# Interim weight bits held in PSUM, layer-2 groups of 6, 5 and 5 blocks, single-step activations and a wider reciprocal spread in a fused attention and two-layer FFN kernel

## The chip, the cores and the metric

The kernel runs on one core of one Trainium2 chip. The metric is the device time of one execution in microseconds, as the median of several executions. The engines are TensorE (PE in the profile; its weight loads are PEld), VectorE (DVE), ScalarE (ACT), GpSimd (POOL) and SyncE (SP), which issues all the transfers of this kernel. [...]

## What is computed

Attention with a learned relative-position bias, then two feed-forward layers with different activations. Cut to what matters:

```python
scores = scale * q @ k.T + bias          # bias: small MLP of log1p|i-j| / log1p(i)
attn   = softmax(scores)                 # row sums, + 1e-9, then divide
x = (attn @ v)                           # 1152 tokens x 512
h = x @ w_in;  g = h * clip(h + 3, 0, 6) / 6;  x = g @ w_out         # layer 1, d_ff 2048
h = x @ w_in2
P = a0 + a1 h + a2 h^2 + a3 h^3;  Q = 1 + |b0||h| + |b1| h^2
out = (P / (Q + 1e-6)) @ w_out2                                       # layer 2, d_ff 2048
```

The inputs are float64. The kernel gets them as pairs of 32-bit words, so each weight block (128 x 512 numbers) arrives as 128 x 1024 words and has to be turned into float32 by integer operations on its bits.

## The kernel before, in words

**Attention.** Eight heads and two batches in five chunks of queries. TensorE computes bias sums (L418), scores (L450, L465), transposes of the exponentials (L655), the product with v (L485), and two small things per chunk: a transpose of the reciprocals of the row sums (L704) and their spread over 128 partitions (L728, `spread_rc`): per batch eight matmuls of 128 columns against a constant 0/1 matrix `sel`. `x_scaled` (L735) multiplies the attention output by that spread. ScalarE and VectorE share the bias units (table `U_ENG`), the copies out of PSUM (`EV_ENG`, `OUT_ENG`) and one VectorE operation adds bias to the scores (L473).

**Feed-forward layers.** Every float32 operand is split in two parts, high and low, and each product is three matmuls (high*high, high*low, low*high). The 16 blocks of d_ff are handled in groups (`FGROUPS`): layer 1 in groups of 3, 5, 4, 4 blocks, layer 2 in groups of 5, 5, 6. Within a group the three token chunks of 384 tokens follow each other; a step is one block and one chunk, so each layer has 48 steps, numbered 0 to 47 and 48 to 95. A step is: twelve matmuls into a PSUM bank `h` (L317, pool of four banks), the activation, the split of its result (ACT L883, then DVE or POOL L891), and the back product into banks `y` (L962; layer 1 uses four banks of 384 columns, layer 2 three of 512). After a group's last step for a chunk, `y_out` (L988, L990, L992) adds the `y` banks to the sums in SBUF, and at the end of layer 2 sends them out (L994).

**Layer 2's activation**, per step: ACT `abs` L899, `q` L906, `u` L912; POOL `qq` L918; DVE `step_uu` L924 and L925 back to back; ACT logarithm L931 and exponential L936; DVE `step_div` L942, L943, L944 back to back; then ACT L883 and POOL L891. The `h` bank is free again after L944.

**Weights.** An item is one weight block, 64 in all; the fourth block's number of an item is its side (in or out). `w_load` (L794) brings the words into a buffer of the tag `big` (11 of them). `w_bits` makes float32 in three VectorE operations on one tile `wk` in SBUF: L267 reads the high words and writes `wk`; L269 reads the high words and `wk` and writes `wk`; L271 reads the low words and `wk` and writes `wk`. Then ACT L813 makes the high part and POOL L822 the low part, in a home that `w_home` picks: the first four items of a group in one of two `huge` buffers, seven items of the even groups in `wp`, the rest in `big`.

**Order.** The tile framework runs with a manual schedule: a list of small pieces of work (`plan`), each issuing a few instructions, is run through in the order of the table `ORDER`. Every engine works through its own instructions strictly in that order. Buffers and banks are taken from a pool where the piece that needs one is run, and wait for the reader that last held them.

Of the kernel before, what the change touches and what calls it, by code (L numbers as in the profile page):

```python
# [33 lines left out]
FGROUPS = (((0, 3), (3, 8), (8, 12), (12, 16)), ((0, 5), (5, 10), (10, 16)))  # L34
NWP = 7
NPAIR = NH // 2
U_ENG = (0, 0, 1, 0, 0, 0, 1, 0, 1, 0, 0, 0, 1, 0, 0, 0, 0, 0, 1, 0, 0, 0, 0, 0, 0, 0, 0, 0, 1, 0, 0, 0, 0, 0, 1, 0, 0,
# [7 lines left out]
OUT_ENG = (0, 0, 0, 0, 0, 0, 0, 0, 0, 0, 0, 0, 0, 0, 1, 1, 0, 1, 1, 1)  # L45
X_DVE = (0, 0, 0, 0, 1, 0, 0, 0, 1)
PTX = (1,) * 20 + (0,) * 20
N_EARLY = 5
# [1032 lines left out]
```

## Time and profile before

| what | us |
|---|---|
| median of 3 runs | 622.6 (620.86 to 623.19) |
| the profiled execution | 622.65 |
| its span in the profile | 620.9 |
| PE busy | 591.9 |
| DVE busy | 491.8 |
| ACT busy | 397.8 |
| POOL busy | 207.8 |

The profile is of the execution with 622.65 us; 1.75 us of it lie outside the span. "Busy" is the time in which an engine had some instruction under way. Matmuls overlap each other, so the duration of one is longer than the distance from one to the next; where the prediction prices matmuls it takes the length of a run of them. The same holds in a small way for VectorE, whose next operation starts before the row of the last one ends.

### The profile page before, as it was taken

The numbers are of one execution on the slowest core, as the hardware profiler recorded it, in microseconds if no ns is written. First come the engines' busy times: TensorE is split into PE (matmuls) and PEld (weight loads), VectorE is DVE, ScalarE is ACT, GpSimd is POOL, SyncE is SP. The second block draws the span as 40 slices with busy tenths as digits, with TensorE's granted clock in tenths as the row PEclk, the third lists the DMA queues.
The fourth block names the chain that finished last, engine by engine and source line by source line (L and its number), as shares of the span: only waits on it lengthen the run. The fifth ranks groups of instructions, "written<-read, shape, count | busy, mean of one in ns | idle before, by whom it ended". The sixth has DMA issues, their size and how long they took to land.

```text
span 620.9 us, 11361 instructions
## 1 busy us (share of the span) xinstructions
PE 591.9 (95%) x4342; PEld 516.9 (83%) x4342; DVE 491.8 (79%) x926; ACT 397.8 (64%) x833; POOL 207.8 (33%) x184
## 2 busy tenths in 40 slices
PE   8989999999999999999999999979979898969996
PEld 5457777777789999999999999968868787958885
DVE  7978787665767774567576679998999899999973
ACT  6968888887784634233333347668867777567981
POOL 1000100100034533022221213555757856567651
PEclk9999999999999999999999999999979999979999
DMA  7993224124344424072221324301012224000102
GB/s 244 250 231 95 64 59 118 52 77 113 106 114 160 135 78 129 2 235 77 94 68 43 94 96 142 102 34 35 34 35 68 69 93 145 1 1 1 52 28 75
DMA packets 31974, 56.63 MB, mean 91 GB/s; under 512 B 2472, under 2 KB 18984, under 8 KB 31920
## 3 DMA queue, kind: packets, MB, share of 16 engines
q1 hardware_dynamic: 31920, 55.91, 30.3%
q8 instruction: 34, 0.56, 0.4%
q14 instruction: 20, 0.16, 0.1%
HBM read 41.75 MB, written 2.36 MB: 71 GB/s over the span
## 4 chain that ended last, share of the span: by engine, by line
PE 62%; DVE 27%; ACT 4%; DMA 4%; issue 1%; SPq 0%; POOL 0%; ACTq 0%; POOLq 0%
PE h L317 20%; PE y L962 19%; PE h L485 6%; PE h L655 6%; PE ps L450 5%; DVE wk L269 4%; DVE wk L271 4%; PE h L418 4%; DVE e L925 3%; DVE e L944 3%; DVE e L942 3%; DVE h L943 3%; DVE e L924 2%; DVE wk L267 2%; DMA huge<-wk 2%; DMA vraw<-in_v_dram 2%
## 5 line engine op out<-in xcount | busy, mean ns | idle before, releaser
L317 PE MATMUL h<-xt,huge 128*128 128x384 f32 x504 | 95.4, 337 | 0.1
L317 PEld LDWEIGHTS h<-xt,huge 128*128 128x128 f32 x504 | 89.0, 189 | 2.3 <-DVE e L944 0.8
L822 POOL TENSOR_TENSOR huge<-wk,huge 128x512 fp32r<-128x512 f32 x28 | 39.3, 1404 | 98.8 <-ACT huge L813 95.8
L891 POOL TENSOR_TENSOR gl<-e,gh 128x384 fp32r<-128x384 f32 x48 | 50.0, 1041 | 57.9 <-ACT gh L883 52.4
L473 DVE CUSTOM_DVE_ANT_0 big<-ps,huge 128x576 f32<-128x576 f32 (+1 forms) x72 | 52.4, 761 | 17.5 <-PE ps L450 16.1
L269 DVE SCALAR_TENSOR_TENSOR wk<-big,wk 128x512 int32<-128x512 int32 x64 | 63.9, 1004 | 0.7
L317 PE MATMUL h<-xt,big 128*128 128x384 f32 x324 | 62.2, 341 | 2.3 <-DVE e L944 2.3
L918 POOL TENSOR_TENSOR e<-e,e 128x384 f32<-128x384 f32 x48 | 54.7, 1143 | 22.4 <-ACT e L906 22.3
L317 PE MATMUL h<-xt,wp 128*128 128x384 f32 x324 | 60.8, 336 | 1.0 <-DVE e L944 1.0
L317 PEld LDWEIGHTS h<-xt,big 128*128 128x128 f32 x324 | 57.9, 192 | 4.3 <-DVE e L944 3.6
L866 ACT ACTIVATE e<-h,cons 128x384 f32<-128x384 f32 x43 | 25.0, 581 | 55.7 <-PE h L317 55.7
L317 PEld LDWEIGHTS h<-xt,wp 128*128 128x128 f32 x324 | 57.0, 188 | 3.0 <-DVE e L944 1.6
L755 POOL TENSOR_TENSOR xt<-oT,xt 128x512 fp32r<-128x512 f32 x7 | 8.9, 1280 | 145.4 <-ACT xt L749 145.4
L637 ACT ACTIVATE big<-big,mx 128x576 f32<-128x576 f32 (+1 forms) x72 | 56.1, 790 | 2.1 <-DVE mx L473 2.1
L271 DVE SCALAR_TENSOR_TENSOR wk<-big,wk 128x512 int32<-128x512 int32 x64 | 56.2, 884 | 0.2
L883 ACT ACTIVATE gh<-h 128x384 fp32r<-128x384 f32 x43 | 21.1, 492 | 47.7 <-PE y L962 45.8
L411 DVE TENSOR_SCALAR big<-psw,thr 128x576 f32<-128x576 f32 x104 | 47.5, 517 | 2.9 <-PE h L418 2.6
L962 PE MATMUL y<-huge,gh 128*128 128x512 f32 x108 | 34.9, 424 | 12.3 <-DVE part L990 8.5
L883 ACT ACTIVATE gh<-e 128x384 fp32r<-128x384 f32 x48 | 25.1, 523 | 29.1 <-DVE e L944 28.6
L655 PEld LDWEIGHTS h<-csm,big 128*128 128x128 f32 x328 | 35.4, 142 | 10.0 <-issue 7.1
L655 PE MATMUL h<-csm,big 128*128 128x128 f32 x328 | 41.2, 277 | 1.6 <-ACT wk L426 1.2
L418 PE MATMUL h<-big,wblk 128*32 128x288 f32 x576 | 40.7, 410 | 1.9 <-ACT wk L426 0.9
(120 smaller groups left out, 1310.6 us busy)
## 6 DMA issues: line engine op xcount, KB each, us to landing
big<-in_moe_w_in_dram SPq DMA_DIRECT2D x32, 512.0 KB, 4.0
big<-in_moe_w_out_dram SPq DMA_DIRECT2D x32, 512.0 KB, 3.5
huge<-wk SPq DMA_DIRECT2D x40, 288.0 KB, 4.0
kraw<-in_k_dram SPq DMA_DIRECT2D x4, 576.0 KB, 9.4
rawq<-in_q_dram SPq DMA_DIRECT2D x4, 512.0 KB, 6.8
vraw<-in_v_dram SPq DMA_DIRECT2D x8, 256.0 KB, 8.2
out_dram<-part SPq DMA_DIRECT2D x5, 256.0 KB, 2.5
out_dram<-psw SPq DMA_DIRECT2D x3, 256.0 KB, 2.5
```

What stands on the lines that cost most here:

```text
L269: nc.vector.scalar_tensor_tensor(wt, high, -0x40000000, wt, op0=ALU.bitwise_and, op1=ALU.bitwise_or)
L271: nc.vector.scalar_tensor_tensor(wt, low, 29, wt, op0=ALU.logical_shift_right, op1=ALU.bitwise_or)
L317: nc.tensor.matmul(ps, wx[:, c, :], xx[:, c, :], start=(i == c == 0), stop=(i == 2 and c == KC - 1))
L411: eng.tensor_scalar(dst, win, thr[:, g:g + 1], 0.0, op0=ALU.add, op1=ALU.max)
L418: nc.tensor.matmul(ps[32 * ct:32 * ct + 32, :HS], wblk.rearrange("p i h -> p (i h)"), units_of[G, ct][:, hf * HS:(hf + 1) * HS], start=Tru ...
L473: nc.vector.tensor_tensor_reduce(ss, ps, biases[qc][:, h * S:h * S + n], op0=ALU.add, op1=ALU.min, scale=-0.125, scalar=3e38, accum_out=mx)
L637: nc.scalar.activation(ss, ss, AF.Exp, bias=mxs[u // 2][:, b, u % 2:u % 2 + 1], scale=-1.0, accum_out=sums[qc][:, b, h:h + 1])
L655: nc.tensor.transpose(ps[:, c - c0], pes[u][:, c * P:(c + 1) * P], ident)
L883: nc.scalar.activation(gs[j][0], hs[j] if L == 0 and j >= N_EARLY else act[j], AF.Copy)
L891: eng.tensor_tensor(gl, src, gh.bitcast(F32), op=ALU.subtract)
L918: nc.gpsimd.tensor_tensor(vq, vq, ab, op=ALU.mult)
L962: nc.tensor.matmul(ys[c][d][:, :TC if L == 0 else DM], lhs, rhs, start=(first and i == 0), stop=(last and i == 2))
```

## The change

**Interim bits in PSUM.** The first two operations of `w_bits` write a tile `mid`, and only the third writes `wk`. For the six items of the first group `mid` is that same `wk`, as before. For all other items it is a bank of PSUM: one of the four `h` banks up to the fourth item of group 5 (layer 2's second group), from there on one of the four `y` banks, of which layer 2 uses three at a time.

**Groups and homes.** Layer 2's groups are 6, 5, 5. The last two groups keep their last four items in `huge` instead of the first four, and `wp` takes other items.

**Single steps.** `step_uu` is cut into `um` and `uu`, `step_div` into `p`, `r` and `div`; the same five VectorE operations, each with its own place in the order.

**Spread.** `spread_rc` runs per half of the head pairs instead of per batch: four matmuls of 256 columns (both batches) in place of eight of 128. The last chunk has one batch's worth of rows and stays at eight of 128 columns. `x_scaled` follows in halves.

**Order and tables.** `ORDER`, `U_ENG`, `EV_ENG`, `OUT_ENG` and `X_DVE` are new. Of the 144 bias units 33 are on ACT (before 28), of 120 copies of pieces 78 on ACT (before 86). When the first layer-2 step (48) is issued, 40 of the 64 items have their bits made (before 36); the last item's bits come between steps 82 and 83 (before 86 and 87).

```diff
-FGROUPS = (((0, 3), (3, 8), (8, 12), (12, 16)), ((0, 5), (5, 10), (10, 16)))
+FGROUPS = (((0, 3), (3, 8), (8, 12), (12, 16)), ((0, 6), (6, 11), (11, 16)))
-X_DVE = (0, 0, 0, 0, 1, 0, 0, 0, 1)
+X_DVE = (0, 0, 0, 0, 0, 0, 1, 0, 1)
...
-    def to_bits(wt, words, i):
+    def to_bits(wt, mid, words, i):
         low, high = words[:, :, :, 0], words[:, :, :, 1]
         if i == 0:
-            nc.vector.tensor_scalar(wt, high, 3, 0x3FFFFFFF, op0=ALU.logical_shift_left, op1=ALU.bitwise_and)
+            nc.vector.tensor_scalar(mid, high, 3, 0x3FFFFFFF, op0=ALU.logical_shift_left, op1=ALU.bitwise_and)
         elif i == 1:
-            nc.vector.scalar_tensor_tensor(wt, high, -0x40000000, wt, op0=ALU.bitwise_and, op1=ALU.bitwise_or)
+            nc.vector.scalar_tensor_tensor(mid, high, -0x40000000, mid, op0=ALU.bitwise_and, op1=ALU.bitwise_or)
         else:
-            nc.vector.scalar_tensor_tensor(wt, low, 29, wt, op0=ALU.logical_shift_right, op1=ALU.bitwise_or)
+            nc.vector.scalar_tensor_tensor(wt, low, 29, mid, op0=ALU.logical_shift_right, op1=ALU.bitwise_or)
...
+    def in_huge(gi, i):
+        j = i - (0 if gi < 5 else len(items(gi)) - 4)
+        return j if 0 <= j < 4 else None
+
+    def in_wp(gi, i):
+        return (gi == 2 and i >= 4) or (gi == 4 and 4 <= i < 11) or (gi == 6 and 2 <= i < 6)
...
-        def spread_rc(qc, b):
+        def spread_rc(qc, k):
             need(("rcs", qc), "sel")
-            ps = BANK((P, KC, P))
-            for hp in range(NPAIR):
+            n = nb_of(qc)
+            ps = BANK((P, 2, 2, P))[:, :, :n]
+            for e in range(2):
+                hp = 2 * k + e
                 for i in range(2):
-                    nc.tensor.matmul(ps[:, hp], sel[:, hp * P:(hp + 1) * P], rcs[qc][:, i, b], start=(i == 0), stop=(i == 1))
+                    nc.tensor.matmul(ps[:, e], sel[:, hp * P:(hp + 1) * P], rcs[qc][:, i, :n], start=(i == 0), stop=(i == 1))
...
         def w_bits(it, i):
             need(("raw", it), *((("bits", it, i - 1),) if i else ()))
             if i == 0:
-                held["wt", it] = W([P, KC, P], I32)
-            to_bits(held["wt", it], held["raw", it], i)
+                where = "h" if it[0] < 5 or (it[0] == 5 and it[1] < 4) else "y"
+                if where == "y":
+                    need("y")
+                held["mid", it] = W([P, KC, P], I32) if it[0] == 0 else T(pools[where], [P, KC, P], I32, where)
             if i == 2:
-                del held["raw", it]
+                held["wt", it] = held["mid", it] if it[0] == 0 else W([P, KC, P], I32)
+            to_bits(held.get(("wt", it)), held["mid", it], held["raw", it], i)
...
+        def step_um(j):
+            need(("u1", j))
+            nc.vector.tensor_tensor(act[j], act[j], hs[j], op=ALU.mult)
+            done.add(("um", j))
...
+        def step_p(j):
+            need(("exp", j))
+            nc.vector.scalar_tensor_tensor(act[j], act[j], acoef[:, 0:1], hs[j], op0=ALU.add, op1=ALU.mult)
+            done.add(("p", j))
...
-                for i, fn in enumerate((step_abs, step_q, step_u, step_qq, step_uu, step_ln, step_exp, step_div)):
-                    at(t + .1 + .1 * i, fn, j)
+                for i, fn in enumerate((step_abs, step_q, step_u, step_qq, step_um, step_uu, step_ln, step_exp, step_p, step_r, step_div)):
+                    at(t + .1 + .09 * i, fn, j)
```

What this does to VectorE in the middle of layer 2: before, around step 63. `wk` and `big` are in SBUF, `e` is an activation buffer in SBUF, `h` a PSUM bank.

```order
L267 TENSOR_SCALAR wk_5262<-big_5115 128x512
L271 SCALAR_TENSOR_TENSOR wk_5215<-big_5056,wk_5215 128x512
L942 SCALAR_TENSOR_TENSOR e_1013_5191<-e_1013_5191,acoef_59,h_5118 128x384
L943 SCALAR_TENSOR_TENSOR h_5118<-e_1004_5149,h_5118 128x384
L944 SCALAR_TENSOR_TENSOR e_1013_5191<-h_5118,e_1013_5191 128x384
L269 SCALAR_TENSOR_TENSOR wk_5262<-big_5115,wk_5262 128x512
L267 TENSOR_SCALAR wk_5300<-big_5163 128x512
L271 SCALAR_TENSOR_TENSOR wk_5262<-big_5115,wk_5262 128x512
```

The same place after, around step 59. L275, L277, L279 are the three operations on the bits, L947 and L952 the two of `um` and `uu`, L968, L973 and L978 those of `p`, `r` and `div`.

```order
L275 TENSOR_SCALAR y_5062<-big_4876 128x512
L277 SCALAR_TENSOR_TENSOR y_5062<-big_4876,y_5062 128x512
L279 SCALAR_TENSOR_TENSOR wk_5079<-big_4876,y_5062 128x512
L968 SCALAR_TENSOR_TENSOR e_1021_5031<-e_1021_5031,acoef_59,h_4994 128x384
L973 SCALAR_TENSOR_TENSOR h_4994<-e_1023_5035,h_4994 128x384
L947 TENSOR_TENSOR e_1033_5085<-e_1033_5085,h_5038 128x384
L978 SCALAR_TENSOR_TENSOR e_1021_5031<-h_4994,e_1021_5031 128x384
L952 SCALAR_TENSOR_TENSOR e_1033_5085<-e_1033_5085,acoef_59,h_5038 128x384
```

The interim result now lies in a `y` bank, no bit operation has two inputs in SBUF, and the operations of two neighbouring steps alternate.

TensorE at the end of the first chunk of queries, before: the bias sums, the spread, the next scores.

```order
L418 MATMUL h_912<-big_756,wblk_89 32x288 x2
L728 MATMUL h_920<-rcT_863,sel_78 128x128 x8
L728 MATMUL h_934<-rcT_863,sel_78 128x128 x8
L450 MATMUL ps_213_947<-kraw_79,rawq_361 128x288
L450 MATMUL ps_214_948<-kraw_79,rawq_361 128x288
```

And after (L434, L746 and L466 are the same three lines).

```order
L434 MATMUL h_912<-big_751,wblk_89 32x288 x2
L746 MATMUL h_920<-rcT_866,sel_78 128x256 x4
L746 MATMUL h_931<-rcT_866,sel_78 128x256 x4
L466 MATMUL ps_213_939<-kraw_79,rawq_357 128x288
L466 MATMUL ps_214_940<-kraw_79,rawq_357 128x288
```

The spread stands in the same place of the row with half as many matmuls, each twice as wide.

## Rows read from the trace of the kernel before

**Rows 1.** Windows: stretch, its length, busy PE, PEld, DVE, ACT, POOL, PE clock, DMA

```profile
45.00:187.00 142.00, 141.50 (x1721) 107.86 (x1720) 102.13 (x251) 118.33 (x284) 13.03 (x12) 1.00 0.32 90
187.00:385.00 198.00, 198.00 (x1177) 197.61 (x1177) 137.80 (x234) 81.17 (x157) 52.76 (x40) 1.00 0.33 105
385.00:568.00 183.00, 165.52 (x796) 145.66 (x794) 176.38 (x282) 131.45 (x258) 114.53 (x98) 0.96 0.16 52
```

**Rows 2.** Chain of work that ended last: start us, us, what

```profile
190.88 8.55 PE h L317 x48
199.43 2.08 PE y L962 x12
...
385.56 1.39 DVE part L990 x3
...
568.05 2.36 PE h L317 x12
...
593.41 2.10 PE h L317 x12
595.52 2.08 PE y L962 x9
...
614.88 2.05 DVE part L992 x3
```

**Rows 3.** Windows: one of two such of 20 us, columns as in rows 1

```profile
440.00:460.00 20.00, 16.75 (x71) 14.59 (x70) 19.32 (x30) 14.21 (x28) 12.95 (x11) 0.83 0.16 53
```

**Rows 4.** Timeline in layer 2, VectorE and GpSimd: start us, us, what

```profile
560.17 0.60 DVE L942 SCALAR_TENSOR_TENSOR e<-e,acoef,h 128x384 f32<-128x384 f32 x1
...
562.48 1.02 POOL L891 TENSOR_TENSOR gl<-e,gh 128x384 fp32r<-128x384 f32 x1 [1.06 <-ACT gh L883]
562.87 1.18 DVE L269 SCALAR_TENSOR_TENSOR wk<-big,wk 128x512 int32<-128x512 int32 x1
563.45 1.47 POOL L918 TENSOR_TENSOR e<-e,e 128x384 f32<-128x384 f32 x1
563.96 1.24 DVE L267 TENSOR_SCALAR wk<-big 128x512 int32<-128x512 int32 x1
565.12 0.68 DVE L271 SCALAR_TENSOR_TENSOR wk<-big,wk 128x512 int32<-128x512 int32 x1
565.73 0.68 DVE L269 SCALAR_TENSOR_TENSOR wk<-big,wk 128x512 int32<-128x512 int32 x1
...
566.54 1.28 POOL L822 TENSOR_TENSOR wp<-wk,wp 128x512 fp32r<-128x512 f32 x1 [1.63 <-ACT wp L813]
```

**Rows 5.** VectorE's groups between 385 and 568 us: count, busy us, mean ns

```profile
L269 DVE SCALAR_TENSOR_TENSOR wk<-big,wk 128x512 int32<-128x512 int32 x27 | 28.8, 1077 | 0.0
L271 DVE SCALAR_TENSOR_TENSOR wk<-big,wk 128x512 int32<-128x512 int32 x26 | 27.7, 1078 | 0.0
...
L267 DVE TENSOR_SCALAR wk<-big 128x512 int32<-128x512 int32 x27 | 18.0, 680 | 0.0
```

**Rows 6.** Single lines over the whole span: duration ns min/median/max, first and last start

```profile
L267 DVE TENSOR_SCALAR wk<-big x64: 404/418/1509, 164.3 to 564.0; 128x512 int32<-128x512 int32 x64
...
L943 DVE SCALAR_TENSOR_TENSOR h<-e,h x48: 546/553/556, 382.8 to 608.5; 128x384 f32<-128x384 f32 x48
...
L992 DVE SCALAR_TENSOR_TENSOR psw<-y,psw x3: 679/681/684, 575.6 to 579.5; 128x512 f32<-128x512 f32 x3
```

**Rows 7.** The chain of work again, in attention

```profile
67.95 1.93 PE h L728 x16
...
71.05 2.12 PE h L655 x18
```

**Rows 8.** TensorE's waits: whom for, us in total, times, longest

```profile
PE y L962 <- DVE part L990: 8.5, 4, 4.9
PE h L317 <- DVE e L944: 3.3, 4, 1.2
```

**Rows 9.** The page's 40 equal slices of the span: what the transfers moved

```profile
GB/s 244 250 231 95 64 59 118 52 77 113 106 114 160 135 78 129 2 235 77 94 68 43 94 96 142 102 34 35 34 35 68 69 93 145 1 1 1 52 28 75
```

More of the change, by code (lines that the diff above doesn't have):

```diff
@@ L33 @@
 HS = S // 2
-FGROUPS = (((0, 3), (3, 8), (8, 12), (12, 16)), ((0, 5), (5, 10), (10, 16)))
+FGROUPS = (((0, 3), (3, 8), (8, 12), (12, 16)), ((0, 6), (6, 11), (11, 16)))
 NWP = 7
 NPAIR = NH // 2
-U_ENG = (0, 0, 1, 0, 0, 0, 1, 0, 1, 0, 0, 0, 1, 0, 0, 0, 0, 0, 1, 0, 0, 0, 0, 0, 0, 0, 0, 0, 1, 0, 0, 0, 0, 0, 1, 0, 0,
[3 rows of a table removed]
-EV_ENG = (1, 0, 1, 1, 1, 0, 1, 1, 0, 1, 1, 0, 1, 0, 1, 1, 1, 1, 1, 0, 1, 1, 1, 1, 1, 0, 0, 1, 1, 1, 1, 0, 1, 1, 1, 1, 1,
[3 rows of a table removed]
-OUT_ENG = (0, 0, 0, 0, 0, 0, 0, 0, 0, 0, 0, 0, 0, 0, 1, 1, 0, 1, 1, 1)
-X_DVE = (0, 0, 0, 0, 1, 0, 0, 0, 1)
+U_ENG = (0, 0, 1, 1, 0, 0, 0, 0, 1, 1, 0, 0, 0, 0, 0, 0, 1, 1, 0, 0, 0, 0, 0, 0, 0, 0, 1, 0, 0, 0, 0, 0, 0, 0, 1, 0, 0,
[3 rows of a table added]
+EV_ENG = (1, 1, 1, 1, 1, 1, 1, 0, 1, 1, 1, 0, 1, 1, 0, 1, 1, 1, 0, 1, 0, 1, 1, 1, 0, 0, 1, 1, 1, 1, 0, 1, 0, 1, 1, 1, 0,
[3 rows of a table added]
+OUT_ENG = (0, 0, 1, 0, 0, 0, 0, 0, 0, 0, 0, 0, 0, 0, 1, 1, 0, 1, 1, 0)
+X_DVE = (0, 0, 0, 0, 0, 0, 1, 0, 1)
 PTX = (1,) * 20 + (0,) * 20
 N_EARLY = 5
-ORDER = (0, 25, 1, 26, 2, 3, 27, 28, 5, 4, 21, 30, 32, 23, 38, 24, 31, 40, 33, 39, 46, 34, 41, 48, 54, 42, 47, 35, 49,
[115 rows of a table removed]
+ORDER = (0, 25, 1, 23, 24, 26, 2, 3, 27, 28, 4, 5, 21, 30, 32, 38, 31, 33, 39, 40, 46, 34, 48, 41, 47, 318, 49, 35, 54,
[123 rows of a table added]
 NWK = 5
@@ L278, in items @@
         return [(gi, 2 * (f - f0) + s, L * NF + f, bool(s)) for f in range(f0, f1) for s in range(2)]
+    def in_huge(gi, i):
[3 more added lines that the diff above has]
+        return (gi == 2 and i >= 4) or (gi == 4 and 4 <= i < 11) or (gi == 6 and 2 <= i < 6)
     def w_home(gi, i):
-        if i < 4:
-            if i == 0:
+        j = in_huge(gi, i)
+        if j is not None:
+            if j == 0:
                 home[gi] = HUGE([P, 4, 2, KC, P], F32R)
-            return home[gi][:, i]
-        if gi % 2 == 0 and gi > 0 and i < 4 + NWP:
+            return home[gi][:, j]
+        if in_wp(gi, i):
             return T(pools["e"], [P, 2, KC, P], F32R, "wp", bufs=NWP)
@@ L721, in recips_low, with x_scaled @@
             done.add(("rcs", qc))
-        def spread_rc(qc, b):
+        def spread_rc(qc, k):
             need(("rcs", qc), "sel")
-            ps = BANK((P, KC, P))
-            for hp in range(NPAIR):
+            n = nb_of(qc)
+            ps = BANK((P, 2, 2, P))[:, :, :n]
+            for e in range(2):
+                hp = 2 * k + e
                 for i in range(2):
-                    nc.tensor.matmul(ps[:, hp], sel[:, hp * P:(hp + 1) * P], rcs[qc][:, i, b], start=(i == 0), stop=(i == 1))
-            held["bc", qc, b] = ps
-            done.add(("bc", qc, b))
-        def x_scaled(qc, b):
-            need(("bc", qc, b), *(("o", 4 * qc + hp) for hp in range(NPAIR)))
-            o = oT[qc][:, b]
-            nc.vector.tensor_tensor(o, o, held.pop(("bc", qc, b)), op=ALU.mult)
-            done.add(("xs", qc, b))
+                    nc.tensor.matmul(ps[:, e], sel[:, hp * P:(hp + 1) * P], rcs[qc][:, i, :n], start=(i == 0), stop=(i == 1))
+            held["bc", qc, k] = ps
+            done.add(("bc", qc, k))
+        def x_scaled(qc, k):
+            need(("bc", qc, k), *(("o", 4 * qc + hp) for hp in (2 * k, 2 * k + 1)))
+            o = oT[qc][:, :nb_of(qc), 2 * k:2 * k + 2]
+            nc.vector.tensor_tensor(o, o, held.pop(("bc", qc, k)).rearrange("p e b t -> p b e t"), op=ALU.mult)
+            done.add(("xs", qc, k))
         def x_parts(qc, b):
@@ L743, in x_high @@
             c, t = divmod(PLACE[2 * qc + b], 3)
-            need(("xs", qc, b), *((("x room", c),) if t else ()))
+            need(("xs", qc, 0), ("xs", qc, 1), *((("x room", c),) if t else ()))
             if t == 0:
@@ L781, in fused_kernel @@
                 at(t + .16, recips_low, qc)
+                for half in range(2):
+                    at(t + .4 + .03 * half, spread_rc, qc, half)
+                    at(t + .45 + .01 * half, x_scaled, qc, half)
                 for b in range(nb_):
-                    at(t + .4 + .1 * b, spread_rc, qc, b)
-                    at(t + .45 + .1 * b, x_scaled, qc, b)
                     at(t + .5 + .1 * b, x_high, qc, b)
@@ L800, in w_bits @@
             if i == 0:
-                held["wt", it] = W([P, KC, P], I32)
-            to_bits(held["wt", it], held["raw", it], i)
+                where = "h" if it[0] < 5 or (it[0] == 5 and it[1] < 4) else "y"
+                if where == "y":
+                    need("y")
+                held["mid", it] = W([P, KC, P], I32) if it[0] == 0 else T(pools[where], [P, KC, P], I32, where)
             if i == 2:
-                del held["raw", it]
+                held["wt", it] = held["mid", it] if it[0] == 0 else W([P, KC, P], I32)
+            to_bits(held.get(("wt", it)), held["mid", it], held["raw", it], i)
+            if i == 2:
+                del held["raw", it], held["mid", it]
                 done.add(("wt", it))
@@ L809, in w_high @@
             gi, i, n, out_side = it
-            need(("wt", it), *((("home", gi),) if 0 < i < 4 else ()), *(("attention",) if 4 <= i < 4 + NWP and gi % 2 == 0 and gi else ()))
+            need(("wt", it), *((("home", gi),) if in_huge(gi, i) else ()), *(("attention",) if in_wp(gi, i) else ()))
             pair = w_home(gi, i)
@@ L813, in w_high @@
             nc.scalar.activation(pair[:, 0], held["wt", it].bitcast(F32), AF.Copy)
-            if i == 0:
+            if in_huge(gi, i) == 0:
                 done.add(("home", gi))
@@ L919, in step_qq @@
             done.add(("q2", j))
+        def step_um(j):
+            need(("u1", j))
+            nc.vector.tensor_tensor(act[j], act[j], hs[j], op=ALU.mult)
+            done.add(("um", j))
         def step_uu(j):
-            need(("u1", j))
-            u, ps = act[j], hs[j]
-            nc.vector.tensor_tensor(u, u, ps, op=ALU.mult)
-            nc.vector.scalar_tensor_tensor(u, u, acoef[:, 1:2], ps, op0=ALU.add, op1=ALU.mult)
+            need(("um", j))
+            nc.vector.scalar_tensor_tensor(act[j], act[j], acoef[:, 1:2], hs[j], op0=ALU.add, op1=ALU.mult)
             done.add(("u2", j))
@@ L937, in step_exp, with step_r @@
             done.add(("exp", j))
-        def step_div(j):
-            need(("exp", j))
-            u, ps, vq = act[j], hs[j], more[j][1]
-            nc.vector.scalar_tensor_tensor(u, u, acoef[:, 0:1], ps, op0=ALU.add, op1=ALU.mult)
-            nc.vector.scalar_tensor_tensor(ps, vq, 1.0 + 1e-6, ps, op0=ALU.add, op1=ALU.mult)
-            nc.vector.scalar_tensor_tensor(u, ps, -2.0, u, op0=ALU.add, op1=ALU.mult)
+        def step_p(j):
+            need(("exp", j))
+            nc.vector.scalar_tensor_tensor(act[j], act[j], acoef[:, 0:1], hs[j], op0=ALU.add, op1=ALU.mult)
+            done.add(("p", j))
+        def step_r(j):
+            need(("p", j))
+            nc.vector.scalar_tensor_tensor(hs[j], more[j][1], 1.0 + 1e-6, hs[j], op0=ALU.add, op1=ALU.mult)
+            done.add(("r", j))
+        def step_div(j):
+            need(("r", j))
+            nc.vector.scalar_tensor_tensor(act[j], hs[j], -2.0, act[j], op0=ALU.add, op1=ALU.mult)
             done.add(("g", j))
```

250 rows, old and new, of tables (EV_ENG, ORDER, U_ENG) are left out of this document.

## The prediction

> **What bounds the kernel now.** I read the windows first, stage by stage, then the chain of work that ended last, then the timeline where the chain leaves TensorE. In attention and in layer 1 TensorE has no room: it is busy for 141.50 of 142 us and for 198.00 of 198 us [rows 1]. In the next 183 us, up to 568, that turns round: VectorE is busy for 176.38 us and TensorE for 165.52. The chain says the same: TensorE's products back to back from 190.88 on, VectorE from 385.56, TensorE again from 568.05 to the last product at 614.88 [rows 2].
>
> How much TensorE loses there: a step's twelve `h` matmuls and its `y` matmuls take 2.08 us each in layer 1 and 2.10 + 2.08 = 4.19 together in layer 2 (starts of the rows) [rows 2]. From 190.88 there are 47 + 48 such pieces left of layer 1 and 48 pairs of layer 2: 95 x 2.08 + 48 x 4.19 = 398.7 us. They take 614.88 - 190.88 = 424.0. So 25.3 us are lost, and since layer 1 shows no idle time, all of it in layer 2 before 568. [...]
>
> Why VectorE is late: the weight bits. L269 and L271 take 1.08 us on average in that stretch and L267 0.68 [rows 5], but a neighbour of the same shape takes 0.68 where GpSimd is idle [rows 4]. The timeline shows the mechanism: L269 starts at 562.87 beside GpSimd's L891, which ends at 563.50, and ends 0.55 us behind it; L267 starts at 563.96 beside L918, which ends at 564.92, and ends 0.28 us behind it. Each stands until GpSimd's operation is over and then does its work. L943, which has one input in SBUF and one in PSUM, shows nothing of that: 546 to 556 ns over 48 instructions, though GpSimd is busy for 114.53 of the 183 us [rows 1, 6].
>
> **The bits.** The change removes the second SBUF input from L269 and L271 and the SBUF output from L267 and the second operation. What they then cost: the second has L943's operands (SBUF and PSUM in, PSUM out), 552 ns for 384 columns; at 512 columns the like is L992 with PSUM input, 681 ns [rows 6]. Starts of neighbours lie 0.61 us apart for 0.68 us rows [rows 4], so 0.61 each. For the first operation, SBUF in and PSUM out, no row stands: 0.36 from below (404 ns, as it is alone, less the same overlap) and 0.69 from above (L992's whole row); I take 0.60, near the rows with PSUM. An item then costs VectorE 1.82 us. Before it costs, in this stretch, 0.68 + 1.08 + 1.08 less 0.07 overlap each = 2.63 us.
>
> The trace shows no fixed price for PSUM: 681 ns against 680 for two SBUF inputs alone [rows 4, 6]. [...]
>
> **VectorE against TensorE in layer 2.** The five operations of an activation step take 562.87 - 560.17 = 2.70 us from start to start [rows 4]; before and after alike. I count in the order of either kernel what stands between the first layer-2 step on TensorE and the last back product before the bits are all done. Before (up to step 83): 39 steps' worth of activations 105.1, other VectorE work (sums of `y`, second layer's input) 17.7, 28 items x 2.63 = 73.6: 196 us, against 173 us of TensorE (83 pieces of 2.08). The 23 us of surplus answer to the 25.3 lost, so the count can be trusted to some 2 us. After (up to step 80): activations 95, other work 13, 24 items x 1.82 = 43.5: 151.5 us, against 152 us of TensorE (73 pieces). By groups and chunks: 17.9 against 14.6 up to step 47, 21.4 against 25.0 (53), 24.2 against 25.0 (59), 25.2 against 25.0 (65), 20.1 against 20.8 (70), 22.0 against 20.8 (75), 20.7 against 20.8 (80), then VectorE has slack. Only the first piece puts VectorE behind, by 3.3 us, since four items move up to there; the later ones even out. So VectorE stops being the limit, and TensorE is next. I put the loss at 3.3 + 2, about 5 us in place of 25.3: **20.3 us less**. Bounds: 0 us lost (TensorE never waits), 11 if each bit operation costs L992's whole row of 0.69 (24 x 3 x 0.08 = 6 more).
>
> Four of the 28 items go into layer 1: 4 x 1.82 us of VectorE, which is busy there for 137.80 of 198 us [rows 1]; nothing on the path. The bits in layer 1 take one of the four `h` banks for three operations. In layer 2 a step holds its bank over some ten operations of three engines and TensorE still waits for one only 3.3 us in all [rows 8]; in layer 1 a step holds it over four. So a bank is spare there, and the wait costs nothing; without that cover see the last rival. The cut into single steps adds no instruction; it puts other work between operations that depend on each other, a gain or loss of at most the 0.07 us by which rows overlap, taken as nothing.
>
> **The spread.** For the first four chunks of queries it is 16 matmuls of 128 columns, 1.93 us, 121 ns each [rows 7], now 8 of 256. TensorE is full there, so the path feels it. Price of 256 columns: a layer-1 matmul of 384 takes 173 ns [rows 2] and a transpose of 128 takes 118 [rows 7], so 121 from below and 173 from the next wider; 242 if the time grows with the columns. A piece that hardly changes from 118 to 173 between 128 and 384 columns is nearest to 121. 8 x 0.121 = 0.97, a gain of 0.96 x 4 = **3.9 us** (0 to 3.9). The last chunk stays. Other tables (`U_ENG`, `EV_ENG`) trade some operations between ACT (118 of 142 us) and DVE (102 of 142) [rows 1], covered by TensorE.
>
> **The start.** Among SyncE's transfers the last block of k (576 KB) moves behind four more transfers of bias rows, and the 320 KB of the late bias table move ahead of v. The first three slices move 231 to 250 GB/s [rows 9], so the one makes what stands behind it up to 2.4 us earlier and the other 1.3 us later; taken as nothing, 1.5 either way. The new order issues seven `h` pieces ahead of the first back product; TensorE is busy all the same.
>
> **Sum.** 622.65 (the profiled execution, 0.05 above the median) - 20.3 - 3.9 = **598.5 us**.
>
> **The rivals.**
>
> *Banks `y` become the wait.* The interim takes the one `y` bank that layer 2 has spare, and at a change of chunk the next products want it. Before, TensorE waited there for VectorE's sums 8.5 us in four waits, up to 4.9 [rows 8], with the spare bank free. Five changes (59, 65, 70, 75, 80) with 2.1 us each are 10.6: 609 us. For it: VectorE runs at the limit there. Against: the order puts the third bit operation ahead of the new chunk's first product, and VectorE's queue in front of the sums is shorter without the stretched operations. Chance 0.19.
>
> *PSUM costs more.* In layer 2, 48 bit operations now read PSUM, and VectorE is just level with TensorE, so what they cost on top goes into the end. From rows the most is a start distance equal to the whole row, 0.68 - 0.61 = 0.07 each, 3.4 us: 602. Against it: L943 and L992 with PSUM operands are no longer than rows of their width without [rows 4, 6]. Chance 0.04. [...]
>
> *The stretch isn't GpSimd's doing*, but comes from reading every second word of `big`, which stays. Then an item keeps 2.63 us, and 24 x 0.81 = 19.5 us come back: 618. Against: the short rows read `big` in the same way [rows 4]. Chance 0.05.
>
> *Slower: `h` banks in layer 1.* TensorE has no slack there, and 34 items take a bank out of four before step 48. A wait for an `h` bank goes whole into the end. The change's gain of 24.2 us is gone from 24.2 / 34 = 0.71 us of wait per item, little over one bit operation; with two operations, 1.2 us, it is 41 lost: 639. Against: the spare bank above, and VectorE idle for 60 of layer 1's 198 us [rows 1], so that it rarely lets an item wait between its operations. Chance 0.06.
>
> **How the numbers follow.** My forecast has 0.66. Its own range is 593 (no wait at all, and the start's 1.5 not lost) to 606 (12 us lost). The range of 8 in 10 goes to 611, to take in the wait for `y`; it leaves out the last two rivals and some of the edges. Faster by over 0.5%, below 619.5, about the least that a measurement of this kernel can tell from no change: 0.66 + 0.19 + 0.04 and most of the 0.05, 0.92. Within it 0.03, slower 0.05.
>
> **What would show it.** In the new profile: the three bit operations near 0.60 to 0.69 us with little spread, whatever GpSimd does; TensorE's clock full in layer 2 and its lost time between the first `h` and the last `y` at about 5 us; the spread at about 1 us per chunk; attention ending some 4 us earlier, layer 1 as long as before. Wrong would be: bit operations of 1 us and more; waits of `y` products for VectorE of over 8 us; waits of `h` in layer 1.

## The result, and the profile after

The changed kernel takes 599.23 us (median of 4 runs, 598.64 to 599.88), the kernel before 622.19 beside it: a ratio of 0.963, 95% interval 0.961 to 0.966. The forecast was 598.5 us, the range 593 to 611. The total was met; the terms for layer 2 and for the start were not, and it is luck that they cancel. The profiled execution took 599.88 us with a span of 598.1. Lines of code have moved: L269 and L271 are now L277 and L279, L267 is L275, `h` is L333, `y` L996, the spread L746, GpSimd's L891, L918 and L822 are L915, L942 and L846. The experiments have line numbers of their own.

Windows of attention, layer 1 and layer 2 (length, busy PE, PEld, DVE, ACT, POOL, clock, DMA share, GB/s), against [rows 1]:

```profile
45.00:183.00 138.00, 135.31 (x1552) 101.00 (x1552) 98.50 (x243) 110.43 (x261) 9.18 (x9) 0.98 0.33 87
183.00:382.00 199.00, 199.00 (x1290) 196.96 (x1285) 139.12 (x252) 82.68 (x166) 54.89 (x43) 1.00 0.34 109
382.00:560.00 178.00, 178.00 (x911) 163.28 (x910) 163.04 (x306) 149.63 (x293) 114.76 (x108) 1.00 0.18 57
```

Layer 2 is TensorE's now: 178.00 of 178 us at a granted clock of 1.00 (before, 0.83 in the 20 us of [rows 3]), VectorE 163.04. The first row is worse than in [rows 1]: 2.7 us idle and a clock of 0.98.

TensorE's waits over the whole span (line, whom for: us, times, longest), against [rows 8]:

```profile
PE h L434 <- ACT wk L442: 2.7, 5, 0.9
PE h L559 <- POOL ones L383: 2.2, 1, 2.2
PE h L671 <- ACT wk L442: 2.0, 3, 1.1
PE h L501 <- DMA vraw<-in_v_dram: 1.1, 2, 1.0
PE ps L466 <- DMA kraw<-in_k_dram: 1.0, 1, 1.0
PE ps L466 <- DVE mx L489: 0.4, 1, 0.4
```

None of these lines belongs to a layer; all are in the first 50 us. The chain of work says the same (start, us, what), against [rows 2]:

```profile
75.04 1.15 PE h L746 x8
...
197.12 10.82 PE h L333 x60
207.94 6.24 PE y L996 x36
...
581.05 2.10 PE h L333 x12
583.15 8.90 PE y L996 x39
592.05 0.02 issue
592.07 2.05 DVE part L1026 x3
```

From 197.12 TensorE runs unbroken to 592.05: the remaining 46 + 48 pieces of layer 1 and 48 pairs of layer 2 are 94 x 2.08 + 48 x 4.19 = 396.6 us by the prediction's prices, and they take 394.9. Counted to the same mark (the start of the last sum, with 1.4 us of products still to go), the kernel before lost 26.7 us and this one nothing.

The bit operations over the whole span, by the place of their output and of the interim (ns min/median/max, first and last start), against [rows 6]:

```profile
L275 DVE TENSOR_SCALAR h<-big x42: 680/686/689, 206.1 to 457.0; 128x512 int32<-128x512 int32 x42
...
L277 DVE SCALAR_TENSOR_TENSOR h<-big,h x42: 681/689/697, 207.1 to 459.1; 128x512 int32<-128x512 int32 x42
...
L279 DVE SCALAR_TENSOR_TENSOR wk<-big,h x42: 675/682/691, 208.2 to 460.1; 128x512 int32<-128x512 int32 x42
```

And a piece of layer 2's timeline, VectorE and GpSimd, against [rows 4]:

```profile
453.97 0.69 DVE L275 TENSOR_SCALAR h<-big 128x512 int32<-128x512 int32 x1
454.69 0.69 DVE L277 SCALAR_TENSOR_TENSOR h<-big,h 128x512 int32<-128x512 int32 x1
454.93 1.02 POOL L915 TENSOR_TENSOR gl<-e,gh 128x384 fp32r<-128x384 f32 x1 [1.22 <-ACT gh L907]
455.42 0.69 DVE L279 SCALAR_TENSOR_TENSOR wk<-big,h 128x512 int32<-128x512 int32 x1
...
457.01 0.69 DVE L275 TENSOR_SCALAR h<-big 128x512 int32<-128x512 int32 x1
457.36 1.30 POOL L846 TENSOR_TENSOR huge<-wk,huge 128x512 fp32r<-128x512 f32 x1
457.61 0.55 DVE L947 TENSOR_TENSOR e<-e,h 128x384 f32<-128x384 f32 x1
```

L277 ends in the middle of GpSimd's L915; L279 starts in its middle and takes 0.69 us all the same; neither waits for its end. The second L275 starts 0.60 us ahead of its neighbour L947 though L846 begins beside it. Where the three operations of an item follow each other directly, as at the top, their starts are 0.72 and 0.73 us apart and not 0.60; what makes this difference no run shows.

What went the other way is the start. The first spread starts at 75.04 us, before at 67.95 [rows 7]; 7.1 us later. The spreads take 1.15 instead of 1.93 us, so four give back 3.1, and attention ends some 4 us later (counted by the pieces of layer 1 that stand behind it), not 4 us earlier. The place is this (windows, and the chain of work there):

```profile
45.00:50.00 5.00, 2.31 (x16) 1.57 (x15) 1.45 (x4) 2.46 (x7) 0.00 (x0) 0.88 1.04 222
50.00:55.00 5.00, 5.00 (x29) 3.63 (x29) 2.74 (x6) 2.38 (x5) 0.00 (x0) 0.50 0.06 22
```

```profile
39.65 7.79 DMA huge<-wk
...
49.24 2.18 PE h L671 x9
51.42 2.22 PE ps L466 x8
53.64 3.31 PE h L501 x40
56.95 1.13 PE h L671 x9
58.08 1.17 PE ps L466 x8
...
63.30 2.33 PE h L501 x40
```

ScalarE's copy L442 waits until a transfer of bias rows (`huge<-wk`) has given back its buffer `wk`, and TensorE waits for ScalarE. TensorE is busy for 2.31 of 5 us, and then works at a granted clock of 0.50 (50 to 55 us). The same pieces at a clock of 1.00 (56 to 63 us and on) are 1.13, 1.17 and 2.33 us (the last three rows): some 1.0 us each lost, 3.1 together.

### The profile page after: what moved, and what is told of

It is laid out like the page before. It is cut to its first block, busy times and chain, and to the rows that moved or that the text cites. A ratio compares the mean times of both kernels' runs of the same rounds, so it can differ in the third digit from the quotient of the medians.

```text
span 598.1 us, 11410 instructions
## 1 busy us (share of the span) xinstructions
PE 583.8 (98%) x4310; PEld 513.1 (86%) x4310; DVE 460.1 (77%) x930; ACT 397.0 (66%) x830; POOL 195.4 (33%) x184
## 4 chain that ended last, share of the span: by engine, by line
PE 91%; DMA 5%; DVE 3%; ACT 1%; issue 0%; SPq 0%; ACTq 0%; DVEq 0%
PE h L333 34%; PE y L996 33%; PE h L501 7%; PE h L671 6%; PE ps L466 5%; DMA huge<-wk 4%; PE h L434 3%; DVE big L427 2%; PE h L746 1%; PE ps L481 1%; DMA psw<-in_cpsi_dram 1%; PE h L720 0%; DVE part L1026 0%; ACT wk L442 0%; PE ps L474 0%
## 5 line engine op out<-in xcount | busy, mean ns | idle before, releaser
L333 PE MATMUL h<-xt,huge 128*128 128x384 f32 x504 | 94.5, 336 | 0.0
L333 PEld LDWEIGHTS h<-xt,huge 128*128 128x128 f32 x504 | 88.4, 188 | 2.0 <-DVE wk L896 0.3
L333 PE MATMUL h<-xt,big 128*128 128x384 f32 x360 | 67.6, 335 | 0.0
L846 POOL TENSOR_TENSOR huge<-wk,huge 128x512 fp32r<-128x512 f32 x28 | 36.7, 1311 | 88.9 <-DVE h L896 69.6
L942 POOL TENSOR_TENSOR e<-e,e 128x384 f32<-128x384 f32 x48 | 49.1, 1023 | 50.2 <-ACT e L930 49.9
L333 PEld LDWEIGHTS h<-xt,big 128*128 128x128 f32 x360 | 63.1, 188 | 0.8
L915 POOL TENSOR_TENSOR gl<-e,gh 128x384 fp32r<-128x384 f32 x48 | 48.9, 1020 | 23.9 <-ACT gh L907 17.9
L333 PE MATMUL h<-xt,wp 128*128 128x384 f32 x288 | 53.8, 335 | 0.0
L333 PEld LDWEIGHTS h<-xt,wp 128*128 128x128 f32 x288 | 50.7, 188 | 1.1
L896 DVE SCALAR_TENSOR_TENSOR h<-e,h 128x384 f32<-128x384 f32 x43 | 24.0, 559 | 29.5 <-ACT e L890 29.5
L466 PE MATMUL ps<-kraw,rawq 64*128 64x288 f32 x256 | 41.4, 438 | 1.3 <-DMA kraw<-in_k_dram 1.0
L434 PE MATMUL h<-big,wblk 128*32 128x288 f32 x576 | 39.5, 410 | 2.8 <-ACT wk L442 2.7
L968 DVE SCALAR_TENSOR_TENSOR e<-e,acoef,h 128x384 f32<-128x384 f32 x48 | 29.3, 610 | 14.5 <-ACT h L963 14.3
L442 ACT ACTIVATE wk<-h,csm 128x288 f32<-128x288 f32 x72 | 32.1, 493 | 10.5 <-PE h L434 5.0
```

Of the source, the lines that this page charges most:

```text
L333: nc.tensor.matmul(ps, wx[:, c, :], xx[:, c, :], start=(i == c == 0), stop=(i == 2 and c == KC - 1))
L434: nc.tensor.matmul(ps[32 * ct:32 * ct + 32, :HS], wblk.rearrange("p i h -> p (i h)"), units_of[G, ct][:, hf * HS:(hf + 1) * HS], start=Tru ...
L466: nc.tensor.matmul(ps[e][:, 512 - HS * (1 - c):512 + HS * c] if c else ps[e][:, 512 - HS:512], x[r, b, hp, :], kraw[r, hp, S * b + HS * c: ...
L846: nc.gpsimd.tensor_tensor(lo, held.pop(("wt", it)).bitcast(F32), hi.bitcast(F32), op=ALU.subtract)
L915: eng.tensor_tensor(gl, src, gh.bitcast(F32), op=ALU.subtract)
L942: nc.gpsimd.tensor_tensor(vq, vq, ab, op=ALU.mult)
```

## The experiments

All are edits of the changed kernel, but for e2 and e8, which are built on the kernel before. The ratio is to the kernel before in the same comparison, with its 95% interval. The last column is the difference of that ratio and the changed kernel's 0.9632, times 622.2 us; each is uncertain by some 2 us.

| run | median, us | ratio to before | against the changed kernel, us |
|---|---|---|---|
| e1_sbuf | 611.62 | 0.983 (0.980 to 0.986) | +12.3 |
| e2_psum_alone | 636.36 | 1.023 (1.020 to 1.026) | +37.0 |
| e3_start | 591.71 | 0.951 (0.949 to 0.953) | -7.6 |
| e4_narrow | 602.44 | 0.969 (0.966 to 0.971) | +3.4 |
| e5_no_gpsimd | 597.89 | 0.959 (0.957 to 0.962) | -2.4 |
| e6_fused | 603.45 | 0.968 (0.965 to 0.970) | +2.8 |
| e7_psit | 597.33 | 0.958 (0.956 to 0.961) | -3.0 |
| e8_old_layer2 | 622.49 | 1.000 (0.998 to 1.002) | +22.8 |
| e9_engines | 599.51 | 0.962 (0.959 to 0.965) | -0.7 |
| e10_l1_sbuf | 598.74 | 0.961 (0.957 to 0.964) | -1.6 |
| e11_coef | 594.99 | 0.955 (0.952 to 0.958) | -5.1 |
| e12_loads | 592.54 | 0.950 (0.948 to 0.953) | -8.0 |

**e1: the bits back in SBUF.**

```diff
...
-                held["mid", it] = W([P, KC, P], I32) if it[0] == 0 else T(pools[where], [P, KC, P], I32, where)
+                held["mid", it] = W([P, KC, P], I32)
             if i == 2:
-                held["wt", it] = held["mid", it] if it[0] == 0 else W([P, KC, P], I32)
+                held["wt", it] = held["mid", it]
```

> The changed kernel with one edit: the interim bits of every weight go back into an SBUF buffer (wk) instead of a PSUM bank; order, groups, single steps and spread stay. Theory (VectorE's bit operations stretch when GpSimd works beside them and all their operands lie in SBUF): in layer 2 the first and third bit operations take 1.0 to 1.1 us again in the mean instead of 0.68, TensorE loses 15 to 27 us there, and the time is 614 to 626 us. Rival (the new order and the groups of 6, 5, 5 gave the time back, the place of the bits is incidental): the operations may stretch, but the time stays at 598 to 603 us.

Neither: +12.3 us, between the two. VectorE's groups from 382 to 560 us (count, busy us, mean ns):

```profile
L277 DVE SCALAR_TENSOR_TENSOR wk<-big,wk 128x512 int32<-128x512 int32 x24 | 26.2, 1094 | 0.3
L279 DVE SCALAR_TENSOR_TENSOR wk<-big,wk 128x512 int32<-128x512 int32 x24 | 24.5, 1020 | 0.1
...
L275 DVE TENSOR_SCALAR wk<-big 128x512 int32<-128x512 int32 x23 | 17.8, 779 | 0.0
```

The window of the same stretch:

```profile
382.00:560.00 178.00, 168.25 (x840) 150.94 (x839) 171.99 (x286) 136.97 (x271) 120.53 (x100) 0.99 0.17 55
```

The operations stretch as they did before [rows 5], and TensorE is busy for 168.25 of these 178 us instead of 178.00. So the banks do what they were thought to do, but they are worth 12 us in this order, not all of the 26.7.

**e5: the same without GpSimd beside the bits.**

On top of e1's edit:

```diff
...
-            nc.gpsimd.tensor_tensor(lo, held.pop(("wt", it)).bitcast(F32), hi.bitcast(F32), op=ALU.subtract)
+            held.pop(("wt", it))
+            ws[n, out_side] = hi, hi
...
-            nc.gpsimd.tensor_tensor(vq, vq, ab, op=ALU.mult)
```

> The kernel of e1 (interim bits in SBUF, 611.6 us, bit operations of 779, 1112 and 1020 ns in layer 2) with GpSimd's work in the two layers left out: the low halves of all weights and of layer 2's gated values are not subtracted, TensorE reads the high half in their place (same number of matmuls), and the square in layer 2's activation is not taken. VectorE's and ScalarE's instructions are the same. Theory (the operations stretch since GpSimd works beside them on SBUF): the three take 0.40 to 0.45, 0.66 to 0.70 and 0.66 to 0.70 us with hardly any spread, TensorE does not wait in layer 2, and the time is 597 to 600 us. Rival (operands in SBUF are slow for these operations by themselves, as three passes over words of 8 bytes): they stay above 0.9 us, and the time at 607 us or more.

The same groups as in e1:

```profile
L279 DVE SCALAR_TENSOR_TENSOR wk<-big,wk 128x512 int32<-128x512 int32 x24 | 16.4, 684 | 0.1
L277 DVE SCALAR_TENSOR_TENSOR wk<-big,wk 128x512 int32<-128x512 int32 x24 | 16.4, 686 | 0.3
L275 DVE TENSOR_SCALAR wk<-big 128x512 int32<-128x512 int32 x23 | 9.6, 419 | 0.0
```

```profile
382.00:560.00 178.00, 178.00 (x911) 163.28 (x910) 158.20 (x307) 148.00 (x295) 0.00 (x0) 1.00 0.17 55
```

All in SBUF, and no stretch: 0.69 and 0.68 us instead of 1.09 and 1.02, 0.42 instead of 0.78. TensorE is busy for 178.00 of 178 us. The stretch is GpSimd's doing, not the step of 8 bytes in `big`; that rival falls.

**e2 and e8: banks without the new layer 2.** e2 is the kernel before with banks. e8 has the changed kernel's start and layer 1, and the kernel before's layer 2, with banks. What both edit in `w_bits` of the kernel before (which bank `where` names differs: e2 leaves eight items of layer 2's first group in SBUF, e8 gives every item behind the first group a bank):

```diff
-                held["wt", it] = W([P, KC, P], I32)
-            to_bits(held["wt", it], held["raw", it], i)
...
+                held["mid", it] = T(pools[where], [P, KC, P], I32, where) if where and it[0] else W([P, KC, P], I32)
             if i == 2:
-                del held["raw", it]
+                held["wt", it] = W([P, KC, P], I32) if it in banked else held["mid", it]
...
+            to_bits(held.get(("wt", it)), held["mid", it], held["raw", it], i)
```

> The kernel before with one part of the change: the interim bits of 44 of its 58 weight items after the first group go into PSUM banks or stay there where a bank is free (groups 2 to 4 of layer 1 and groups 2 and 3 of layer 2, and the last two out-side items of layer 2's first group; eight items of that first group stay in SBUF), with the bit operations of one item closed before the next item opens. Groups of 5, 5, 6, fused steps, narrow spread and the start are those of before. Theory: the operations in banks take 0.68 us, layer 2 loses 3 to 8 us instead of 26.7, and the time is 600 to 606 us. Rival (order and groups did it): 617 to 623 us.

> Start, attention and layer 1 in the order of the changed kernel, all interim bits in PSUM banks, but layer 2 as before: groups of 5, 5, 6 with their weight homes, fused activation steps and the order of before from layer 2's first h on (with the bit operations of one item closed before the next opens), and the narrow spread. Theory after e1 and e2 (banks give back some 12 of the 27 us that layer 2 lost, groups and order the rest): 613 to 620 us. Rival (banks alone are enough for layer 2, e2 lost its time in layer 1 only): 602 to 607 us.

By e2's trace 50 of the 58 items have their bits in banks (26 in `h`, 24 in `y`), not 44. e2 is slower than the kernel before, by 2.3%, which neither side had expected. TensorE's largest wait is one that neither kernel has:

```profile
PE h L317 <- DVE gl L900: 11.4, 6, 2.6
```

It is layer 1 without a free `h` bank (L900 is this run's L891, which reads an `h` bank last). My reading is that in the order of before an `h` piece comes where the bits hold one of the four; but e2 also closes the bits of an item before the next opens, and what that has of the wait no run separates. The operation on the second layer's last input starts at 432.3 us instead of 411.3. From there to the start of the last sum e2 takes 195.6 us and the kernel before 203.6, so its second layer does gain. The wait is the prediction's slower rival, in the order that was not written for banks.

e8 has layer 1 without a wait, and bit operations of 0.69 us in layer 2. Its groups from 382 to 560 us, and its waits in the layers (L1000 is its sum of a `y` bank, L954 the last operation of its division):

```profile
L268 DVE TENSOR_SCALAR y<-big 128x512 int32<-128x512 int32 x23 | 15.9, 692 | 0.6
L270 DVE SCALAR_TENSOR_TENSOR y<-big,y 128x512 int32<-128x512 int32 x22 | 15.2, 692 | 0.4
L272 DVE SCALAR_TENSOR_TENSOR wk<-big,y 128x512 int32<-128x512 int32 x22 | 15.0, 683 | 0.5
```

```profile
PE y L972 <- DVE part L1000: 6.7, 4, 3.4
PE h L318 <- DVE e L954: 6.0, 4, 3.6
```

```profile
382.00:560.00 178.00, 165.23 (x813) 147.75 (x812) 155.59 (x275) 132.83 (x260) 100.90 (x95) 0.97 0.19 58
```

VectorE is busy for 155.59 us of 178, so idle for 22.4, and TensorE still waits 12.8 us and the clock is 0.97. What is late is not VectorE as a whole, but, as I read it, a sum or an activation behind other work at the wrong moment; whether the 6.7 us on `y` come of late sums or of the bits that hold the spare bank, no run separates. My theory on e8 was short by 2.5 us at its upper end; its rival falls.

By the ratios, layer 2's loss is now known for four cases. For the kernel before: 22.9 us against the changed one, less 3.1 for the spread, and 7.8 more for its better start (e3, e12), 27.6. For e8: 22.8 less 3.1, 19.7. The chains, counted to the same mark as above, agree: 26.7 for the kernel before, 20.0 for e8, 13.6 for e1.

| layer 2 loses, us | bits in SBUF | bits in banks |
|---|---|---|
| groups, steps and order of before | 27.6 | 19.7 |
| groups, steps and order of the change | 12.3 | 0 |

The upper row is not the banks alone: e8 has the changed kernel's layer 1, and with it 24 items' bits in layer 2 instead of 28, and it closes an item's bits in a row. So 7.9 is what banks, four items fewer and that closing give together.

**e6: the single steps fused.**

```diff
         def step_um(j):
             need(("u1", j))
-            nc.vector.tensor_tensor(act[j], act[j], hs[j], op=ALU.mult)
...
         def step_uu(j):
             need(("um", j))
+            nc.vector.tensor_tensor(act[j], act[j], hs[j], op=ALU.mult)
```

(and `step_p` and `step_r` moved into `step_div` in the same way)

> The changed kernel with layer 2's activation in the steps of before: the product and the sum over it in one planned step, and the three operations ahead of the division's end in one, so that VectorE issues them in a row; order and places are otherwise those of the changed kernel. Theory (with the bits in banks VectorE has room: 163 us of work in 178 us): 599 to 603 us. Rival (the single steps are what lets bits and sums be served in time): TensorE waits again for y or h in layer 2, 604 to 612 us.

+2.8 us; 603.45 lies between the end of the theory and the begin of the rival, and the rival's sign is there: TensorE waits for VectorE's sums in layer 2 again, 2.2 us in two waits, where it did not wait. (The trace is of an execution of 600.22 us, so the waits behind the median of 603.45 may be longer.) A small part of the new order's 15 to 20 us. Whether the rest is the groups of 6, 5, 5 or the order, no run separates: another grouping needs another order.

**e10: layer 1's bits in SBUF, layer 2's in banks.** (`it[0] == 0` becomes `it[0] < 4` in both lines of e1's diff.)

> The changed kernel with the interim bits of all layer-1 weights in SBUF and those of layer 2 in PSUM banks. Theory (VectorE has room in layer 1, 139 us of work in 199, so the stretch costs nothing there; with the bits in SBUF, VectorE had 148.9 us and TensorE did not wait): 598.5 to 601 us, all of the gain of the banks lies in layer 2. Rival (the banks of layer 1 are needed, as what is late there comes through in layer 2): 603 us or more.

No difference that can be told: in this order the banks matter in layer 2 alone.

**e4: the spread in 128 columns.**

```diff
-                for i in range(2):
-                    nc.tensor.matmul(ps[:, e], sel[:, hp * P:(hp + 1) * P], rcs[qc][:, i, :n], start=(i == 0), stop=(i == 1))
+                for b in range(n):
+                    for i in range(2):
+                        nc.tensor.matmul(ps[:, e, b], sel[:, hp * P:(hp + 1) * P], rcs[qc][:, i, b], start=(i == 0), stop=(i == 1))
```

> The changed kernel with the spread of 1/sum in matmuls of 128 columns again (16 for each of the four full chunks instead of 8 of 256). Theory (TensorE has no gap after the start, so each matmul counts in full): by 121 ns against 144 ns for one, 0.78 us for each chunk, 3.1 us in all, the time is 601.5 to 603 us. Rival (the spread stands where TensorE would wait anyway): 599 to 600 us.

+3.4 us against 3.1 by the rows: it counts in full.

**e3: the start of before.** The first 310 entries of `ORDER` and their engines, as in the kernel before.

> The changed kernel with the first 310 planned steps (all before the first spread of 1/sum) in the order and on the engines of the kernel before; from there on the changed order. In the trace of the changed kernel the first spread starts 7.1 us later than before, and attention ends 4.2 us later (with the saving of the wide spread in it). Theory (the order of the start cost these 7 us, since TensorE is busy without a gap afterwards and can't catch up): the time is 591 to 595 us. Rival (the lateness is made up or given back further on, at the second chunk's bias rows or where weights come): 597 to 601 us.

-7.6 us: what the start lost stays lost to the end, and comes back whole. 591.7 us is faster than both kernels.

**e9, e7, e11, e12: what in the start.** Engines alone, psit alone, the two coefficient loads alone, all loads. The edit of the last, in words of the plan, by the order of SyncE's loads:

```diff
-load acoef, load bcoef, load q 0, load k 0, load k 1, load k 2, sel_load
+load q 0, load k 0, load k 1, load k 2, sel_load, load acoef, load bcoef
...
-load_psit (behind load q 1), psit_sign (behind group_out 12)
+load_psit (behind group_out 18), psit_sign (ahead of the first spread)
...
-load k 3 (behind group_out 15)
+load k 3 (behind group_out 11)
```

> The changed kernel in its own order, with the engines of the kernel before for all that stands ahead of the first spread (21 bias units, 9 evictions of transposed pieces, one of a back product change between VectorE and ScalarE). The start of before as a whole (order and engines) gave 591.7 us. Theory (the start is late by its transfers, not by its engines): 597.5 to 600.5 us. Rival (VectorE's and ScalarE's share in the bias units makes it late): 592 to 596 us.

> The changed kernel with two planned steps put back to their place of before: the load of psit (320 KB, issued at 24.6 us instead of 59.8) and VectorE's sign operation on it. Theory 1 (this load ahead of v and of the bias rows is what made the start late, at some 245 GB/s 1.3 us of transfer, and 0.7 us of VectorE): 597 to 598.5 us, a part of the 7.5 us that the start of before gives back. Theory 2 (with it the half-clock stretch from 49.2 to 56.0 us goes too, since TensorE's idle time ahead of it shrinks): 592 to 596 us. Rival (bias units on other engines and the order of their sums made the start late): 598.5 to 600 us.

> The changed kernel with two loads put back: the coefficients of layer 2's activation (2 KB and 1 KB spread over 128 partitions) are issued behind the first transfers of q and k and the one for the spread's selector instead of ahead of q and k, where the moved data fall from 277 to 116 and 126 GB/s for two slices of 2.3 us. Theory (small pieces hold up the queue, and all that the start moves afterwards is later): 595.5 to 598 us. Rival (only q and k are later, and TensorE has other work then): 598.5 to 600 us.

> The changed kernel with all loads of the start in the places of before: the late bias table with its sign operation back (as in e7, 597.3 us), the last block of k ahead of the bias rows, the coefficients behind q and k. Bias units, their engines and sums stay in the changed order. Theory (the transfers make the start late: TensorE waits less ahead of 50 us, and the half-clock stretch there goes with its idle time): 591.5 to 594.5 us, as with the whole start of before. Rival (order and engines of the bias units have a share of their own): 595 to 597.5 us.

The engines make no difference that can be told (-0.7). The late bias table (`psit`) gives back 3.0, the coefficients 5.1, all loads 8.0, as much as the whole start (7.6); for the last block of k nothing is left that can be told. e7 fits its first theory, e9 and e12 theirs; e11 is 0.5 us better than its own. The clock from 45 to 60 us is 0.77 in the changed kernel and 0.89 in e11, and from 45 to 55 it is 1.00 in e12 and e3, so the 3.1 us of the clock are a part of what these give back. Of e7's 3.0 they are not shown to be one: from 50 to 56 us its clock is 0.85, 1.00 and 1.00, but ahead of that it is 0.79 and 0.50 (46 to 50 us), and 0.96 over the first 42 us, where the changed kernel has 1.00. The windows at the begin, of the changed kernel and then of e12:

```profile
4.00:6.00 2.00, 2.00 (x11) 2.00 (x10) 1.76 (x6) 0.18 (x1) 0.00 (x0) 1.00 0.24 72
6.00:8.00 2.00, 2.00 (x13) 2.00 (x12) 2.00 (x6) 2.00 (x4) 0.00 (x0) 1.00 0.57 204
```

```profile
4.00:6.00 2.00, 2.00 (x14) 2.00 (x14) 1.43 (x5) 0.00 (x0) 0.00 (x0) 1.00 0.96 365
6.00:8.00 2.00, 2.00 (x23) 1.88 (x24) 1.97 (x6) 1.80 (x3) 0.00 (x0) 1.00 1.01 388
```

With 3 KB of coefficients ahead of q and k the DMA engines are busy for 0.24 and 0.57 of the two windows instead of 0.96 and 1.01. Over the first 45 us the share is 0.86 and 0.95, a difference of 4 us of transfer, and from 20 to 45 us the DMA engines are full in the changed kernel (1.01 to 1.07 in each window of 5 us) and in the kernel before (1.02 to 1.06). So, as I read it, the gap comes through to the bias rows at 47 us. In e12, TensorE has no idle time and a clock of 1.00 there:

```profile
45.00:50.00 5.00, 5.00 (x62) 3.92 (x59) 3.95 (x10) 3.08 (x7) 0.00 (x0) 1.00 0.11 27
```

## Why the prediction was right, and where not

*The stretch and its cause* held. The three operations take 0.68 to 0.69 us in banks, with 9 to 16 ns between shortest and longest. Starts lie 0.60 us apart (457.01 to 457.61), as in the sum, where other work stands between; an item whose three operations follow each other takes 0.72 + 0.73 + 0.61 = 2.06 us instead of 1.82. e5 shows that GpSimd makes the stretch, e1 that it returns with SBUF.

*The term of layer 2* was mis-sized: 20.3 us against 26.7 by the trace. The loss left was put at 5 us and is none; the lower bound was the value. The other 1.4 us: the kernel before had lost 26.7 us and not the 25.3 that the prediction reads, which counts the products behind 614.88 as done by then.

*The working behind it failed in one step*: "The 23 us of surplus answer to the 25.3 lost, so the count can be trusted to some 2 us." The count of VectorE's work against TensorE's gives e8's layer 2, with the 24 items that its trace shows there, about 105.1 + 17.7 + 24 x 1.82 = 166.5 us against 173 of TensorE, hence no loss; it lost 19.7. It gives e1 24 x 0.81 = 19.5 us, the figure of the third rival; it lost 12.3. So the agreement for the kernel before proved nothing. Of the 27.6 us lost there, banks and four items fewer give 7.9 in the old layer 2; the new groups, steps and order, of which the count knew only that four items move to layer 1, give 15.3 without any bank, and 19.7 with banks, where those items have moved already. Neither is enough alone.

*The spread* was 3.9 and is 3.1: 144 ns for a matmul of 256 columns (1.15 us for 8), not 121. The bounds 121 and 173 held; the middle would have been nearer than the end chosen.

*The start* was "taken as nothing, 1.5 either way" and cost 7 to 8 us. Two of the moved transfers were costed by their size and rate, and the bias table's share came out at 3.0 instead of 1.3. The coefficients' loads, which the change puts ahead of q and k, were left out of the sum, as 3 KB, and cost 5.1. For them size was the wrong measure; for the table 3.0 is uncertain by some 2. A part of the 7 to 8 is the clock: the idle time ahead of 49 us was followed by 6.8 us at a granted clock of 0.53 (49.2 to 56.0 us), 3.1 us lost, which the working did not look for.

*The rivals.* The wait for `y` banks did not come in this order; in e8 TensorE waited 6.7 us for sums, so it is the new layer 2 (groups, steps and order) that keeps it away. The wait for `h` banks in layer 1 is real as well: e2 has it. That PSUM costs more did not show for the two operations that read it: 692 and 683 ns with PSUM operands (e8), 686 and 684 in SBUF alone (e5), 6 ns more for the second operation and 1 less for the third. The whole row from start to start, by which the rival priced them, does stand where an item's operations follow each other (0.72 and 0.73 us), but TensorE waited for none of it (178.00 of 178 us busy). The first operation is dearer in a bank, 686 ns against 419 in e5, and still shorter than the 779 that it takes in e1 beside GpSimd.

So the right total came from 6 us too little for layer 2, 0.8 too much for the spread and 7 left out of the start; that these cancel is luck.

## What to carry to other kernels

When two changes meet (here where data lie, and the order), price each without the other: a count of an engine's work that matches the loss does not show that the work is the cause. Here banks under the old layer 2 (e8) and the new layer 2 without banks (e1) each gave only a part, and banks in an order that was not written for them cost time (e2). At a start that waits for transfers, look at every issue ahead of the large ones: 3 KB cost 5 us here, and the GB/s by slices of 2 us showed it.

## What was not expected of the hardware

Two loads of 2 and 1 KB, spread over 128 partitions and issued ahead of the large ones, left the DMA engines at 72 GB/s for 2 us and 204 for the next 2 (365 and 388 with the loads behind). What holds the transfers up in these 4 us, no run shows.

GpSimd's square in layer 2 gains as well when VectorE's interim bits move to banks. It takes 1124 ns in the mean with the bits in SBUF (e1) and 1023 with banks:

```profile
L939 POOL TENSOR_TENSOR e<-e,e 128x384 f32<-128x384 f32 x48 | 54.0, 1124 | 43.8 <-ACT e L927 41.0
L942 POOL TENSOR_TENSOR e<-e,e 128x384 f32<-128x384 f32 x48 | 49.1, 1023 | 50.2 <-ACT e L930 49.9
```
